# A second table of early tiles, a shorter row prefetch, and a new order of the first loads, in an attention-then-experts kernel

## The chip, the cores and the metric

The kernel runs on one core of one Trainium2 chip, in one launch. The metric is the device time in microseconds (us) of that core. TensorE does the matrix products, VectorE (DVE), ScalarE (ACT) and GpSimd (POOL) the elementwise work, and the SyncE queue (SP) issues most of the DMA transfers; GpSimd issues the indirect ones.

## The reference

Two stages follow each other. First a linear attention with a polynomial sketch:

```python
q_p, k_p = phi(q), phi(k)                 # phi: outer product of two 8-wide projections, 64 features
kv  = einsum('bhsf,bhsd->bhfd', k_p, v)
z   = sum(k_p, axis=2)
attn = einsum('bhsf,bhfd->bhsd', q_p, kv) / (einsum('bhsf,bhf->bhs', q_p, z)[..., None] + 1e-6)
```

with 4 batches, 4 heads, 1088 positions and head size 32. Its output is laid out as 4352 rows x of 128 numbers. Then a mixture of 8 experts, in which each row goes to one expert alone:

```python
e_idx  = argmax(x @ w_gate, axis=1)
gate_w = softmax(x @ w_gate)[e_idx]
out[mask e] = gate_w * sigmoid(x @ w_output_gate)[e] * (relu(x[mask e] @ w1[e]) @ w2[e])
```

w1[e] is 128 x 1024 and w2[e] is 1024 x 128. All is in 32-bit floats.

## The kernel before

**Attention and routing.** The 34 chunks of 128 positions form 9 groups (of 4 chunks, the last of 2). A list of stage names written out by hand, PLAN, sets the program order of everything up to the first expert tiles: each word such as `qa4` or `rd2` calls a small function for one group or route. The groups are bundled in five routes, ROUTES = ((0, 1), (2, 3), (4, 5), (6,), (7, 8)). When a route's attention output is there, stage rc chooses the expert of each row, rp and rs work out a row number in a buffer xs in HBM, and rd (function send) scatters the rows there, one indirect DMA for each chunk (L544). In xs every expert has a region of its own, in which its rows stand in order of arrival. Each row of xs carries 128 numbers, its gate factor and the number of its output row. At the end, stage mp scatters padding rows behind the last row of each expert (L796), so that tiles can be whole.

**Expert tiles.** The experts work on tiles of TS = 128 rows of one expert. Which rows and which expert a tile has is data, so small tables are computed on DVE: eti (expert of each tile) and bti (its first row in xs). SyncE reads a table entry into a register (L626) and issues `rows(t)`, one DMA from xs into a buffer of the ring xin (L632), and `weights(t, a)`, 512 KB each, a = 0 for w1 and a = 1 for w2, into one of NW = 3 buffer pairs wt (L639). The weights are not loaded when the tile three places earlier had the same expert.

**Early tiles.** A tile that is full before all rows have been routed can be started before the end of the attention. The table early_tiles, made behind the second route (MARK = 1, stages mn1 and mt1), holds NE = 9 such tiles: 16 chunks have been routed, and whatever the distribution over the experts, nine tiles are full. Their `rows` need not wait for the later scatters. This is said by groups of instructions that are declared free of dependence on one another ("early"). All other tiles are in the table late_tiles, made behind the last route (mn4, mt4), and their rows wait for every scatter and for the padding. At mt1 the six weight loads of tiles 0 to 2 are issued, and then the nine `rows`.

**The pipeline of tiles.** Five stages make a tile on TensorE and its helpers: tx transposes xin (L803), tv copies the result out of PSUM (L808), tu multiplies by w1 in 16 matmuls (L815), th applies relu (L822), td multiplies by w2 in 16 matmuls (L829), ty scales (L839), and to scatters the tile to the output (L844). Program order on TensorE, once PLAN is done, is that of `step_(t)`:

```python
for w, n in (("tx", t + 2), ("tv", t + 2), ("tu", t + 1), ("th", t + 1), ("td", t), ("ty", t), ("to", t)):
```

Loads are issued where buffers come free: behind tu(t) the first half of the weights of tile t + 3, behind td(t) the second half of the weights of tile t + 3, and then the rows of tile t + NX, NX = 5. SyncE executes its queue in this order, so an entry that waits holds up all that stands behind it. The order in PLAN in which TensorE gets the first tiles is tx0, tx1, tx2, tu0, tx3, tu1, tx4, td0.

Of the kernel before, what the change touches and what calls it, by code (L numbers as in the profile page):

```python
# [13 lines left out]
F32 = mybir.dt.float32  # L14
I32 = mybir.dt.int32
ALU = mybir.AluOpType
# [6 lines left out]
NK, NV, NQ = 4, 5, 2  # L23
TS = 128
NW = 3
NX = 5

# [5 lines left out]
    gt1 qt3 gs1 ql1 gm1 qz1 qc3 ks6 rc0 gc1 ks8 kb6 qa3 kb8 kp6 rg0 rp0 qr3 qt2 rs0 rf0 qs4 qc2 qx3 rd0 kc5 qb4 ql3  # L35
    qp4 kc6 qa2 cl2 qz3 gt2 qr2 kp8 qt4 gs2 qx2 gm2 qc4 qs5 ql2 qz2 gc2 ks7 rc1 qb5 qa4 kb7 qp5 rp1 rg1 kc6 qr4 rs1
    qt5 rf1 mn1 kp7 qs7 qc5 rd1 mt1 qb7 kc7 kc8 qs6 qx4 qb6 ql4 qp6 qa5 cl3 qp7 gt3 qr5 qt6 gs3 qx5 gm3 qc6 qs8 ql5
    qz4 gc3 qt7 qb8 qz5 rc2 qa6 qc7 qa7 qr6 qp8 rg2 qx6 rp2 qr7 ql6 qx7 qt8 ql7 qc8 tx0 rs2 tx1 qa8 tv0 tv1 rf2 tx2
    qr8 tu0 tv2 rd2 qx8 ql8 qz8 tx3 th0 tu1 tv3 qz7 qz6 rc3 tx4 th1 td0 tv4 rg3 rp3 tu2 ty0 rs3 rf3 rc4 td1 th2 rg4
    mn4 tu3 mt4 ty1 rd3 td2 th3 tu4 ty2 rf4 rp4 th4 tx5 rs4 tx6 td3 tv5 tv6 rd4 mp4  # L40
"""
ROUTES = ((0, 1), (2, 3), (4, 5), (6,), (7, 8))
MARK = 1
NOWHERE = 1 << 20


# [5 lines left out]
def kernel(  # L52
# [12 lines left out]
    nc = tc.nc  # L65
# [3 lines left out]
    DM = H * D  # L69
    E = w_d.shape[0]  # L70
# [8 lines left out]
    W = DM + 16  # L79
    CAP = N + TS  # L80
    NT = (N + E * (TS - 1)) // TS
    PR = E * TS // 128

    consts = ctx.enter_context(tc.tile_pool(name="consts", bufs=1))
# [10 lines left out]
    def ring(pool, tag, n, shape):  # L95
        turns[tag] = [pool.tile(shape, F32, tag=f"{tag}{i}", name=f"{tag}{i}") for i in range(n)], [0]

    def nxt(tag):
        bufs, at = turns[tag]
        at[0] += 1  # L100
        return bufs[at[0] % len(bufs)]
# [11 lines left out]
    def apart(group, ins, *others):  # L113

        for g in (group,) + others:
            tc.declare_no_dep(ins.ins, group=g, reason="the rows are distinct")
        tc.add_to_no_dep_group(group, ins.ins)
# [7 lines left out]
    for i, x in enumerate((S1, S2)):  # L125
        own = slice(i * r, (i + 1) * r)
        if wide:
            x, dst, n = x.bitcast(I32), bits[own].rearrange("p d w -> p (d w)"), 2 * D
        else:
            dst, n = plain[own], D  # L130
# [55 lines left out]
    def half(a):  # L186
        return slice(a * FC * 128, (a + 1) * FC * 128)
# [21 lines left out]
    ones = consts.tile([128, 128], F32, tag="ones")  # L209
# [16 lines left out]
    routes = [range(groups[r[0]][0], groups[r[-1]][-1] + 1) for r in ROUTES]  # L226
# [2 lines left out]

    NE = -(-((routes[MARK][-1] + 1) * 128 - E * (TS - 1)) // TS)
    assert 0 < NE <= NT
    ring(consts, "xsT", 3, [128, TS])
    ring(consts, "hT", 2, [128, FC, TS])
    ring(consts, "y", NE + 1, [TS, DM])
    ring(consts, "xin", NE + NX + 2, [TS, W])
    eps = consts.tile([128, 1], F32, tag="eps")
    nc.gpsimd.memset(eps, EPS)
    fresh = {}  # L240
# [15 lines left out]
    pad = consts.tile([128, PR, W], F32, tag="pad")  # L256
# [19 lines left out]
    stepT = consts.tile([128, NT], F32, tag="stepT")  # L276
# [261 lines left out]
    def send(i, ey, sloti, co):  # L538
        n = len(routes[i])
        x = xts.pop(i)  # L540
        nc.gpsimd.tensor_copy(x.bitcast(I32)[:, :n, DM + 1], ids[:, routes[i][0]:routes[i][-1] + 1])
        nc.gpsimd.tensor_mul(x[:, :n, DM], co[:, :n], ey[:, :n, E + 1])  # L542
        for j in range(n):
            apart("rows", nc.gpsimd.indirect_dma_start(  # L544
                out=xs[:, :], out_offset=bass.IndirectOffsetOnAxis(ap=sloti[:, j:j + 1], axis=0),
                in_=x[:, j], in_offset=None, bounds_check=E * CAP - 1), *(["early"] if i > MARK else []))


    eti = consts.tile([128, NT], I32, tag="eti")
    bti = consts.tile([128, NT], I32, tag="bti")  # L550

    def spread(t, n):
        return t[:, :E].unsqueeze(1).to_broadcast((128, n, E))

    def table(t0, n, ends, jump, first, last=None):


        past = consts.tile([128, n, E], F32, tag=f"past{t0}", name="past")
        et = consts.tile([128, n], F32, tag=f"et{t0}", name="et")
        nc.vector.tensor_tensor(past, step[:, :n].unsqueeze(2).to_broadcast((128, n, E)), spread(ends, n), op=ALU.is_ge)  # L560
        with nc.allow_low_precision("numbers of experts are whole"):
            nc.vector.tensor_reduce(eti[:, t0:t0 + n], past[:, :, :E - 1], axis=AX, op=ALU.add)
        nc.vector.tensor_mul(past, past, spread(jump, n))
        nc.vector.tensor_reduce(et, past[:, :, :E - 1], axis=AX, op=ALU.add)
        if last is None:
            nc.vector.tensor_tensor(bti[:, t0:t0 + n], et, stepT[:, :n], op=ALU.add)
        else:

            nc.vector.scalar_tensor_tensor(out=et, in0=et, scalar=first, in1=stepT[:, :n], op0=ALU.add, op1=ALU.add)
            nc.vector.tensor_scalar(bti[:, t0:t0 + n], et, last, None, op0=ALU.min)  # L570

    NS = N // TS
    more = consts.tile([128, 1], I32, tag="more")
    done = consts.tile([128, E + 1], F32, tag="done")
    nc.vector.memset(done, 0.0)
    early = consts.tile([128, E + 1], F32, tag="early")
    nc.vector.memset(early, 0.0)

    def counted():
        ps = psum.tile([128, E], F32, tag="rt", name="ps_n")  # L580
        nc.tensor.matmul(ps, ones, state["carry"], start=True, stop=True)
        return ps

    def early_tiles(ps):
        full = consts.tile([128, E], I32, tag="full")
        jump = consts.tile([128, E], F32, tag="jump")
        nc.vector.tensor_tensor(full, ps, ecap, op=ALU.subtract)
        nc.vector.tensor_single_scalar(full, full, TS.bit_length() - 1, op=ALU.logical_shift_right)
        nc.vector.tensor_tensor_scan(done[:, 1:], ones[:, :E], full, 0.0, op0=ALU.mult, op1=ALU.add)
        nc.vector.tensor_scalar_min(done[:, 1:], done[:, 1:], float(NE))  # L590
        nc.vector.tensor_sub(early[:, :E], done[:, 1:], done[:, :E])
        nc.vector.tensor_scalar(jump, early[:, :E], -float(TS), float(CAP), op0=ALU.mult, op1=ALU.add)
        table(0, NE, done[:, 1:], jump, None)

    def late_tiles(ps):
        num = consts.tile([128, E], F32, tag="num")
# [17 lines left out]
        nc.vector.tensor_tensor_scan(ends, ones[:, :E], nt, 0.0, op0=ALU.mult, op1=ALU.add)  # L614
        nc.vector.tensor_single_scalar(more, ends[:, E - 1:], float(NS - NE), op=ALU.subtract)
        nc.vector.tensor_tensor(jump, early[:, 1:], left, op=ALU.subtract)
# [6 lines left out]
    regs, xin, xTs, hTs = {}, {}, {}, {}  # L623

    def value(tab, t, top):
        return nc.values_load(tab[0:1, t:t + 1], engines=[mybir.EngineType.SP], min_val=0, max_val=top,  # L626
                              skip_runtime_bounds_check_because="the table is made within the bounds")

    def rows(t):
        at = value(bti, t, E * CAP - TS)  # L630
        xin[t] = nxt("xin")
        ins = nc.sync.dma_start(xin[t], xs[bass.ds(at, TS), :])  # L632
        if t < NE:
            tc.add_to_no_dep_group("early", ins.ins)

    def weights(t, a):
        if a == 0:
            regs[t] = value(eti, t, E - 1)
        nc.sync.dma_start(wt[t % NW][a].rearrange("p c x -> p (c x)"),  # L639
                          w_d[bass.ds(regs[t], 1), :, half(a)].rearrange("e p x -> p (e x)"),  # L640
                          cond=regs[t] != regs[t - NW] if t >= NW else None)
# [12 lines left out]
    stages, have, did = {}, {}, set()  # L654
    end = [NT]
# [116 lines left out]
    @stage  # L772
    def rd(i):
        send(i, have.pop(("rg", i)), have.pop(("rs", i)), have.pop(("rf", i)))
# [4 lines left out]

    @stage  # L780
    def mt(i):
        if i == MARK:
            early_tiles(have.pop(("mn", i)))
            for t in range(NW):
                weights(t, 0)
                weights(t, 1)
            for t in range(NE):
                rows(t)
        else:
            late_tiles(have.pop(("mn", i)))  # L790

    @stage
    def mp(i):
        pa, pai = have.pop("pai")
        nc.gpsimd.tensor_copy(pai, pa)
        apart("rows", nc.gpsimd.indirect_dma_start(  # L796
            out=xs[:, :], out_offset=bass.IndirectOffsetOnAxis(ap=pai[:, :1], axis=0),
            in_=pad.rearrange("p a b -> p (a b)"), in_offset=None), "early")

    @stage  # L800
    def tx(t):
# [22 lines left out]
    @stage  # L824
    def td(t):
        hT = have.pop(("th", t))
        ps = have["td", t] = nxt("kvz").rearrange("p a x -> p (a x)")[:, :DM]
        for c in range(FC):
            nc.tensor.matmul(ps, hT[:, c], wt[t % NW][1][:, c], start=(c == 0), stop=(c == FC - 1))  # L829
        if t + NW < end[0]:  # L830
            weights(t + NW, 1)
        if t + NW >= NE - 1:
            for n in range(NE if t + NW == NE - 1 else t + NX, min(t + NX + 1, end[0])):
                rows(n)

    @stage
    def ty(t):
# [85 lines left out]
```

## Time and profile before

The time is 250.34 us, the median of three runs (250.05 to 256.19). The profiled execution has a span of 224.9 us.

| | |
|---|---|
| PE busy | 200.6 us, 89% of the span |
| PE weight loads busy | 194.9 us, 87% |
| DVE / ACT / POOL busy | 31% / 33% / 35% |
| mean granted TensorE clock | 0.958 |
| DMA | 49.10 MB, mean 218 GB/s |
| of it the hardware queue q1 | 43.31 MB in 19,024 packets |
| L815 matmuls | 592, 76.0 us; 592 more on L829, 72.5 us |
| weight loads issued / row fetches issued | 79 / 41 |

37 tiles are worked on, so 592 = 37 x 16. Each busy time adds up the recorded durations of an engine's instructions; a share is a mean over stages that have different limits, so the chain of waits and the timeline are needed to see where time could go. The span is cut into 40 slices, and TensorE's clock falls to half in two places beside the end: in the slices at 62 to 67 us, where the expert tiles begin, and at 101 to 107 us.

### The profile page before, as it was taken

How to read it: one execution, taken by the hardware profiler on the slowest of the kernel's cores; microseconds unless marked ns; L12 is line 12 of the kernel's file. 1: busy time of each engine (PE TensorE's matmuls, PEld its weight loads, DVE VectorE, ACT ScalarE, POOL GpSimd, SP SyncE). 2: the span in 40 equal slices, each digit the busy share in tenths (PEclk: the TensorE clock that was granted, in tenths of full speed). 3: DMA queues.
4: the chain of work that ended last, by engine and by line, in shares of the span. 5: the costliest groups of instructions: out<-in, count | busy, mean ns of one | idle time of the engine just before them, and what ended most of it. 6: DMA issues, size and time to landing. Idle time of an engine off the chain costs nothing.

```text
span 224.9 us, 6588 instructions
## 1 busy us (share of the span) xinstructions
PE 200.6 (89%) x2458; PEld 194.9 (87%) x2458; DVE 69.3 (31%) x221; ACT 74.0 (33%) x140; POOL 78.8 (35%) x130
## 2 busy tenths in 40 slices
PE   7899999999489999907999999999999999999720
PEld 6889999998379999907999999999999999999720
DVE  4557889999645670000000010101010101010000
ACT  2123343425204343400434343433434343434300
POOL 3700006777037747771131313132222223131310
PEclk9999999999958999995999999999999999999995
DMA  5866512349636989966898789989984686883100
GB/s 160 315 193 225 155 50 77 115 117 357 247 94 175 319 294 282 312 254 197 251 315 322 227 237 319 313 314 312 330 311 143 207 263 189 269 292 114 38 30 1
DMA packets 21634, 49.10 MB, mean 218 GB/s; under 512 B 3466, under 2 KB 9100, under 8 KB 21600
## 3 DMA queue, kind: packets, MB, share of 16 engines
q1 hardware_dynamic: 19024, 43.31, 60.2%
q0 software_dynamic: 2416, 5.33, 6.3%
q8 instruction: 21, 0.34, 0.7%
q14 instruction: 13, 0.11, 0.2%
q10 hardware_dynamic: 160, 0.01, 0.0%
HBM read 51.17 MB, written 5.52 MB: 252 GB/s over the span
## 4 chain that ended last, share of the span: by engine, by line
PE 56%; DMA 22%; issue 9%; POOL 7%; DVE 1%; SPq 0%; POOLq 0%; ACT 0%
PE w L815 22%; PE kvz L829 18%; DMA out_dram<-y,xin 12%; POOL xs L544 7%; PE t L346 5%; DMA xs<-pad,pai 4%; PE w L430 2%; PE kvz L405 2%; DMA xs<-x,sloti 2%; DMA wt<-in_w_dram 2%; DMA xin<-xs 2%; PE t L803 2%; PE w L322 2%; PE w L416 1%; DVE kp L362 1%
## 5 line engine op out<-in xcount | busy, mean ns | idle before, releaser
L815 PE MATMUL w<-xsT,wt 128*128 128x128 f32 x592 | 76.0, 284 | 0.0
L829 PE MATMUL kvz<-wt,hT 128*128 128x128 f32 x592 | 72.5, 276 | 1.5 <-SPq L875 1.5
L815 PEld LDWEIGHTS w<-xsT,wt 128*128 128x128 f32 x592 | 72.8, 201 | 0.0
L829 PEld LDWEIGHTS kvz<-wt,hT 128*128 128x128 f32 x592 | 69.5, 193 | 1.7 <-issue 1.7
L844 POOL DMA_INDIRECT out_dram<-y,xin x37 | 35.9, 970 | 88.1 <-DMA wt<-in_w_dram 46.4
L822 ACT ACTIVATE hT<-w 128x1024 f32<-128x1024 f32 x37 | 37.9, 1023 | 69.2 <-PE w L815 69.2
L808 DVE COPY xsT<-t 128x128 f32<-128x128 f32 x38 | 11.0, 291 | 121.9 <-PE t L803 121.9
L544 POOL DMA_INDIRECT xs<-x,sloti x34 | 33.7, 990 | 12.2 <-issue 8.8
L839 ACT ACTIVATE y<-kvz,xin 128x128 f32<-128x128 f32 x37 | 13.6, 367 | 28.6 <-PE kvz L829 28.6
L803 PE MATMUL t<-ident,xin 128*128 128x128 f32 x38 | 11.0, 295 | 10.3 <-DMA xin<-xs 10.3
L803 PEld LDWEIGHTS t<-ident,xin 128*128 128x128 f32 x38 | 5.6, 150 | 11.1 <-DMA xin<-xs 10.9
L430 PE MATMUL w<-kz,qpT 128*64 128x98 f32 x272 | 13.8, 256 | 0.4 <-ACT b_sb L354 0.4
L430 PEld LDWEIGHTS w<-kz,qpT 128*64 128x64 f32 x272 | 12.4, 142 | 0.9 <-ACT b_sb L354 0.5
L542 POOL TENSOR_TENSOR x<-co,ey 128x8 f32<-128x8 f32 (+2 forms) x5 | 1.1, 223 | 33.5 <-DVE rc L447 23.7
L422 ACT COPY qpT<-w 128x1024 f32<-128x1024 f32 (+1 forms) x9 | 8.7, 965 | 9.9 <-PE w L416 9.9
L362 DVE TENSOR_TENSOR qp<-t,b_sb 128x1024 f32<-128x1024 f32 (+1 forms) x9 | 10.4, 1160 | 3.0 <-ACT b_sb L354 2.8
L362 DVE TENSOR_TENSOR kp<-t,b_sb 128x1024 f32<-128x1024 f32 (+1 forms) x9 | 10.4, 1160 | 2.9 <-PE kvz L405 1.8
L405 PE MATMUL kvz<-vt,kp 128*64 128x65 f32 (+1 forms) x288 | 10.5, 223 | 0.0
L346 PE MATMUL t<-Sb,kT 128*64 128x64 f32 x272 | 9.8, 224 | 0.8 <-DVE kp L362 0.5
L354 ACT COPY b_sb<-t 128x128 f32<-128x128 f32 (+1 forms) x18 | 4.7, 259 | 16.4 <-PE t L346 16.1
L346 PEld LDWEIGHTS t<-Sb,kT 128*64 128x64 f32 x272 | 8.7, 138 | 1.6 <-DVE kp L362 0.6
L405 PEld LDWEIGHTS kvz<-vt,kp 128*64 128x64 f32 (+1 forms) x288 | 9.4, 137 | 0.5 <-issue 0.2
(130 smaller groups left out, 120.8 us busy)
## 6 DMA issues: line engine op xcount, KB each, us to landing
wt<-in_w_dram SPq DMA_DIRECT2D x79, 512.0 KB
xin<-xs SPq DMA_DIRECT2D x41, 72.0 KB
vt<-in_v_dram SPq DMA_DIRECT2D x8, 260.0 KB
kT<-in_k_dram SPq DMA_DIRECT2D x8, 256.0 KB
qT<-in_q_dram SPq DMA_DIRECT2D x8, 256.0 KB
out_dram<-y,xin POOLq DMA_INDIRECT x37, 4.7
xs<-x,sloti POOLq DMA_INDIRECT x34, 4.4
vt<-in_v_dram SPq DMA_DIRECT2D x1, 130.0 KB
```

Of the source, the lines that this page charges most:

```text
L346: nc.tensor.matmul(ps[64 * t:64 * (t + 1), j * H:(j + 1) * H], src[:, j * 128 + 64 * t:j * 128 + 64 * (t + 1)], Sb[i], start=i == 0 and j ...
L362: nc.vector.tensor_mul(res[:, :n], bview(av, [list(av.ap[1]), list(av.ap[2]), [0, r]]), bview(bv, [list(bv.ap[1]), [0, r], list(bv.ap[2])]))
L405: nc.tensor.matmul(acc[b][64 * h:64 * (h + 1), s], kp[p0:p0 + np_, j * H + 2 * s + h].rearrange("s i j -> s (i j)"), vt[p0:p0 + np_, j, s] ...
L430: nc.tensor.matmul(ps[64 * t:64 * (t + 1), 2 * j + s, :VG], qpT[:, 2 * j + s, 64 * t:64 * (t + 1)], kz[(c * 128 + 64 * t) // S][:, s], sta ...
L544: apart("rows", nc.gpsimd.indirect_dma_start(out=xs[:, :], out_offset=bass.IndirectOffsetOnAxis(ap=sloti[:, j:j + 1], axis=0), in_=x[:, j] ...
L803: nc.tensor.transpose(have["tx", t], xin[t][:, :DM], ident)
L808: nc.vector.tensor_copy(have["tv", t], have.pop(("tx", t)))
L815: nc.tensor.matmul(ps[:, c], wt[t % NW][0][:, c], xT, start=True, stop=True)
L822: nc.scalar.activation(have["th", t], have.pop(("tu", t)), ACTF.Relu)
L829: nc.tensor.matmul(ps, hT[:, c], wt[t % NW][1][:, c], start=(c == 0), stop=(c == FC - 1))
L839: nc.scalar.activation(have["ty", t], have.pop(("td", t)), ACTF.Copy, scale=xin[t][:, DM:DM + 1])
L844: apart("out", nc.gpsimd.indirect_dma_start(out=out, out_offset=bass.IndirectOffsetOnAxis(ap=x.bitcast(I32)[:, DM + 1:DM + 2], axis=0), in ...
```

## The change

A second table of early tiles is made behind the third route (stages mn2 and mt2, MARKS = (1, 2)). After 24 chunks, 17 tiles are full, so tiles 9 to 16 come from this table and need only the scatters of the first three routes. The late table holds what is left. The groups of independent instructions become early0 and early1, one for each table. NX goes from 5 to 4, so that the rows of tile 17, the first of the late table, are asked for just behind the weights of tile 16. At mt1 the loads are issued tile by tile: both weight halves of tile t, for t below 3, and then its rows. So the weights of tiles 1 and 2 now stand in SyncE's queue behind the first row fetch and its wait. The rings y and xin grow from 10 to 14 and from 16 to 20 buffers, and three tables are cleared on GpSimd where two were cleared on DVE.

```diff
-NX = 5
+NX = 4
-    ... tx0 rs2 tx1 qa8 tv0 tv1 rf2 tx2
-    qr8 tu0 tv2 rd2 qx8 ql8 qz8 tx3 ...
+    ... tx0 rs2 mn2 tx1 qa8 tv0 tv1 rf2 tx2
+    qr8 tu0 tv2 rd2 mt2 qx8 ql8 qz8 tx3 ...
-MARK = 1
+MARKS = (1, 2)
-    NE = -(-((routes[MARK][-1] + 1) * 128 - E * (TS - 1)) // TS)
+    NES = [-(-((routes[m][-1] + 1) * 128 - E * (TS - 1)) // TS) for m in MARKS]
+    NE = NES[-1]
-    ring(consts, "y", NE + 1, [TS, DM])
-    ring(consts, "xin", NE + NX + 2, [TS, W])
+    ring(consts, "y", 14, [TS, DM])
+    ring(consts, "xin", 20, [TS, W])
@@ send @@
-                in_=x[:, j], in_offset=None, bounds_check=E * CAP - 1), *(["early"] if i > MARK else []))
+                in_=x[:, j], in_offset=None, bounds_check=E * CAP - 1), *(f"early{k}" for k, m in enumerate(MARKS) if i > m))
@@ early_tiles: 16 DVE instructions in place of 11 @@
+        t0, t1 = ([0] + NES)[k:k + 2]
+        was, now = earlies[k:k + 2]
...
+        nc.vector.tensor_tensor(new, full, was[:, :E], op=ALU.subtract)
...
+        nc.vector.tensor_add(now[:, :E], was[:, :E], new)
+        nc.vector.tensor_tensor(jump, was[:, 1:], now[:, :E], op=ALU.subtract)
+        nc.vector.tensor_scalar(jump, jump, float(TS), float(CAP), op0=ALU.mult, op1=ALU.add)
+        nc.vector.tensor_scalar_mul(first, was[:, :1], float(TS))
+        table(t0, t1 - t0, ends[:, 1:], jump, first)
@@ rows @@
-        if t < NE:
-            tc.add_to_no_dep_group("early", ins.ins)
+        for k, n in enumerate(NES):
+            if t < n:
+                tc.add_to_no_dep_group(f"early{k}", ins.ins)
@@ mt @@
-        if i == MARK:
-            early_tiles(have.pop(("mn", i)))
-            for t in range(NW):
-                weights(t, 0)
-                weights(t, 1)
-            for t in range(NE):
+        if i in MARKS:
+            early_tiles(MARKS.index(i), have.pop(("mn", i)))
+        if i == MARKS[0]:
+            for t in range(NES[0]):
+                if t < NW:
+                    weights(t, 0)
+                    weights(t, 1)
                 rows(t)
@@ td @@
-        if t + NW >= NE - 1:
-            for n in range(NE if t + NW == NE - 1 else t + NX, min(t + NX + 1, end[0])):
-                rows(n)
+        if NES[0] <= t + NX < end[0]:
+            rows(t + NX)
```

More of the change, by code (lines that the diff above doesn't have):

```diff
@@ L37 @@
     qt5 rf1 mn1 kp7 qs7 qc5 rd1 mt1 qb7 kc7 kc8 qs6 qx4 qb6 ql4 qp6 qa5 cl3 qp7 gt3 qr5 qt6 gs3 qx5 gm3 qc6 qs8 ql5
-    qz4 gc3 qt7 qb8 qz5 rc2 qa6 qc7 qa7 qr6 qp8 rg2 qx6 rp2 qr7 ql6 qx7 qt8 ql7 qc8 tx0 rs2 tx1 qa8 tv0 tv1 rf2 tx2
-    qr8 tu0 tv2 rd2 qx8 ql8 qz8 tx3 th0 tu1 tv3 qz7 qz6 rc3 tx4 th1 td0 tv4 rg3 rp3 tu2 ty0 rs3 rf3 rc4 td1 th2 rg4
+    qz4 gc3 qt7 qb8 qz5 rc2 qa6 qc7 qa7 qr6 qp8 rg2 qx6 rp2 qr7 ql6 qx7 qt8 ql7 qc8 tx0 rs2 mn2 tx1 qa8 tv0 tv1 rf2 tx2
+    qr8 tu0 tv2 rd2 mt2 qx8 ql8 qz8 tx3 th0 tu1 tv3 qz7 qz6 rc3 tx4 th1 td0 tv4 rg3 rp3 tu2 ty0 rs3 rf3 rc4 td1 th2 rg4
     mn4 tu3 mt4 ty1 rd3 td2 th3 tu4 ty2 rf4 rp4 th4 tx5 rs4 tx6 td3 tv5 tv6 rd4 mp4
@@ L228 @@
     RG = max(len(rs) for rs in routes)
-    NE = -(-((routes[MARK][-1] + 1) * 128 - E * (TS - 1)) // TS)
-    assert 0 < NE <= NT
+    NES = [-(-((routes[m][-1] + 1) * 128 - E * (TS - 1)) // TS) for m in MARKS]
+    NE = NES[-1]
+    assert 0 < NES[0] and NE <= NT
     ring(consts, "xsT", 3, [128, TS])
     ring(consts, "hT", 2, [128, FC, TS])
-    ring(consts, "y", NE + 1, [TS, DM])
-    ring(consts, "xin", NE + NX + 2, [TS, W])
+    ring(consts, "y", 14, [TS, DM])
+    ring(consts, "xin", 20, [TS, W])
     eps = consts.tile([128, 1], F32, tag="eps")
@@ L565, in table @@
         if last is None:
-            nc.vector.tensor_tensor(bti[:, t0:t0 + n], et, stepT[:, :n], op=ALU.add)
+            nc.vector.scalar_tensor_tensor(out=bti[:, t0:t0 + n], in0=et, scalar=first, in1=stepT[:, :n],
+                                           op0=ALU.add, op1=ALU.add)
         else:
@@ L573 @@
     more = consts.tile([128, 1], I32, tag="more")
[L574 to L577, printed above, removed]
+    earlies = [consts.tile([128, E + 1], F32, tag=f"early{k}", name=f"early{k}") for k in range(len(MARKS) + 1)]
+    for x in earlies:
+        nc.gpsimd.memset(x, 0.0)
+    early = earlies[-1]
     def counted():
@@ L582, in counted, with early_tiles @@
         return ps
-    def early_tiles(ps):
-        full = consts.tile([128, E], I32, tag="full")
-        jump = consts.tile([128, E], F32, tag="jump")
+    def early_tiles(k, ps):
+        t0, t1 = ([0] + NES)[k:k + 2]
+        was, now = earlies[k:k + 2]
+        full = consts.tile([128, E], I32, tag=f"full{k}", name="full")
+        new = consts.tile([128, E], F32, tag=f"new{k}", name="new")
+        ends = consts.tile([128, E + 1], F32, tag=f"ends{k}", name="ends")
+        jump = consts.tile([128, E], F32, tag=f"jump{k}", name="jump")
+        first = consts.tile([128, 1], F32, tag=f"first{k}", name="first")
         nc.vector.tensor_tensor(full, ps, ecap, op=ALU.subtract)
+        nc.vector.memset(ends[:, :1], 0.0)
         nc.vector.tensor_single_scalar(full, full, TS.bit_length() - 1, op=ALU.logical_shift_right)
[L589 to L593, printed above, removed]
+        nc.vector.tensor_tensor(new, full, was[:, :E], op=ALU.subtract)
+        nc.vector.tensor_tensor_scan(ends[:, 1:], ones[:, :E], new, 0.0, op0=ALU.mult, op1=ALU.add)
+        nc.vector.tensor_scalar_min(ends[:, 1:], ends[:, 1:], float(t1 - t0))
+        nc.vector.tensor_sub(new, ends[:, 1:], ends[:, :E])
+        nc.vector.tensor_add(now[:, :E], was[:, :E], new)
[3 more added lines that the diff above has]
+        table(t0, t1 - t0, ends[:, 1:], jump, first)
     def late_tiles(ps):
@@ L781, in mt @@
     def mt(i):
-        if i == MARK:
-            early_tiles(have.pop(("mn", i)))
-            for t in range(NW):
-                weights(t, 0)
-                weights(t, 1)
-            for t in range(NE):
+        if i in MARKS:
[5 more added lines that the diff above has]
+                    weights(t, 1)
                 rows(t)
-        else:
+        elif i not in MARKS:
             late_tiles(have.pop(("mn", i)))
@@ L797, in mp @@
             out=xs[:, :], out_offset=bass.IndirectOffsetOnAxis(ap=pai[:, :1], axis=0),
-            in_=pad.rearrange("p a b -> p (a b)"), in_offset=None), "early")
+            in_=pad.rearrange("p a b -> p (a b)"), in_offset=None), *(f"early{k}" for k in range(len(MARKS))))
     @stage
```

## The prediction

> **What bounds the kernel now.** I read the chain that ended last first, because TensorE's 89% busy share is a mean over two halves with different limits. From tile 0 on (62 us) the chain is TensorE's own L815 and L829 work, 1.79 us each and 3.68 us a tile, with one break:
>
> ```profile
> 90.61 0.97 POOL xs L544
> 91.59 0.19 POOL pai L795
> 91.92 0.14 issue
> 92.06 8.63 DMA xs<-pad,pai
> 100.71 1.89 DMA xin<-xs
> 102.64 0.48 PE t L803
> 103.12 3.41 PE w L815 x16
> 106.53 2.04 PE kvz L829 x16
> 108.57 0.11 PE t L803
> 108.68 1.79 PE w L815 x16
> 110.47 1.79 PE kvz L829 x16
> ```
>
> See there: the nine early tiles run out, the first late row tile (tile 9) may be fetched only when the pad scatter has landed (100.71), and TensorE, which ended its last L829 at 95.85 by the timeline, starts again at 102.64. The next tile then costs 3.41 + 2.04 instead of 1.79 + 1.79. The list of waits confirms who waited:
>
> ```profile
> PEld t L803 <- DMA xin<-xs: 10.9, 3, 7.0
> PE t L803 <- DMA xin<-xs: 10.3, 3, 6.8
> ```
>
> Three waits in all: one of 6.8 us here, two of 3.5 us together at the start (62 to 63 us). In the whole steady part, rows are never waited for. How much room they have is in the timeline, which I read next:
>
> ```profile
> 109.45 0.33 SPq L632 DMA_DIRECT2D xin<-xs  x1
> ...
> 110.30 1.95 PE L829 MATMUL kvz<-wt,hT 128*128 128x128 f32 x16
> ...
> 112.09 0.27 PE L803 MATMUL t<-ident,xin 128*128 128x128 f32 x1
> ...
> 113.12 0.33 SPq L632 DMA_DIRECT2D xin<-xs  x1
> ...
> 115.77 0.27 PE L803 MATMUL t<-ident,xin 128*128 128x128 f32 x1
> ```
>
> Stage td of tile 7 ends at 108.57; 0.9 us later SyncE issues the rows of tile 12 (NX = 5), and the transpose of tile 12 is the L803 at 115.77: 6.3 us of room. The L829 at 110.30 is td of tile 8, ending at 112.25; under NX = 4 it is behind this one, at 113.12, that tile 12's rows would go out: 2.65 us of room.
>
> How long they take I read from the trace's DMA packet records. Row packets are the only ones of 576 bytes, 128 a tile, so the end of each tile's last packet can be told:
>
> ```
> rows of tile   issued    last packet ends   took
>  9 (queue empty) 100.71     102.31           1.6
> 12               109.45     113.42           4.0
> 18               131.60     135.60           4.0
> 19 to 26, mean                               4.5
> 28, 29, 30 (tiles 27, 28 load nothing)       2.8, 2.2, 1.9
> 31               179.47     183.25           3.8
> ```
>
> TensorE started 0.35 us after the last packet where it waited (tiles 0, 1 and 9).
>
> **What the Trainium skill says.** "DMA: Bandwidth & Descriptors", section "Queues, rings and completion order": a DMA from SyncE is spread over rings on the 16 engines, and on each engine its descriptors are taken in ring order. So rows issued just behind 512 KB of weights queue behind them on every engine. The trace agrees: 1.6 us with an empty queue, 1.9 to 2.8 around tiles that load nothing, about 4 or more behind two loads. "TensorE: Matmul & The Clock Gate", Part 1: after an idle window of about 3.4 us TensorE drops to half clock. The trace agrees: 3.41 us for sixteen L815 after the gap. The same DMA page's "Specifications" put HBM at about 358 GB/s a core; this trace's windows show up to 412 GB/s from 56 to 58 us, so the measurement decides, but the steady 312 to 330 GB/s of the page's slices is not far from full, as engines are about 94% busy from 131 to 166 us.
>
> **The change part by part.**
>
> *Second table (17 early tiles).* Tiles 9 to 16 need only routes 0 to 2, whose last scatter is issued at about 74.3 us; scatters land 2.3 to 6.3 us after issue (the view of tile xs), so before td of tile 5 asks for tile 9 (about 92 us). Tile 17's rows are asked for by td of tile 13, at the earliest 95.85 + 7 x 3.68 = 121.6 us, 21 us after the pad scatter landed; even doubled, its 8.6 us are hidden. The gap goes: 6.8 us of idle, and (3.41 - 1.79) + (2.04 - 1.79) = 1.9 us of slow clock. **-8.7 us.**
>
> *Its DVE work.* early_tiles has 16 DVE instructions where it had 11; those took 2.4 us (45.75 to 48.14), 0.22 each, so a table now costs about 3.5 us. At mt1 this delays the first weights by 1.1 us; they have until 64.8 us, so nothing. At mt2 the 3.5 us stand on DVE ahead of ql8, which frees the PSUM buffer that tu1 writes; DVE has 4.5 us idle between 62 and 70 us, but not all of it in that place.
>
> *Order of the first loads.* Today 3 MB of weights precede the wait for the scatters, and the scatter issued at 54.87 lands only at 60.15, 5.3 us later. With 1 MB ahead I take the least landing that the trace shows, 2.3 us: rows 0 out at 57.2 and at TensorE 1.9 us later, 59.1, just when its earlier work ends (59.14). But now 1 MB of weights goes ahead of rows 1 and another ahead of rows 2, and tx2 stands before tu0 in the plan. 1 MB at some 350 GB/s (the page's slice at 50 to 56 us, 357) is 3.0 us; SyncE issues each load 0.6 us and each row fetch 0.8 us after the one before, and the first bytes come about 1.2 us after issue. That makes rows 1 ready at about 63.3 and rows 2 at 66.3, against 62.9 and 64.8. tu0 starts 1.7 us later; part of it falls out of the half-clock stretch, and mt2 then holds tu1: td0 ends about 2 us later than now. **+2.0 us** (0 to 3.5).
>
> *NX from 5 to 4.* This is the large term. Call lag the time from the end of td(t) to the last packet of the rows it asks for: 0.9 us to issue plus 3.8 to 4.5, that is 4.7 to 5.4 us with both weight halves loading. The path: td(t) frees a weight buffer, SyncE issues 512 KB into it, then the rows behind it in the ring; tx(t+4) is first on TensorE after td(t+1), with tu(t+3) and td(t+2) queued behind. So lag + 0.35 must fit one step of 3.68 us plus that step's own stall. If each step stalls s, then lag + 0.35 = (3.68 + s) + s, so s = (lag + 0.35 - 3.68) / 2. Lag 4.2, 4.7 and 5.4 give 0.43, 0.69 and 1.03 us. I take 0.7, near the lower measured lag: a stalled TensorE asks for weights less often, so the backlog falls towards that of a load begun on an idle ring (tiles 12, 18, 31). The lowest bound is an empty queue, lag 0.9 + 1.6 = 2.5, and s = 0. It concerns tiles 9 to 36, 28 steps: **+19.6 us** (12 to 29). Stalls under 1.5 us leave no 3.4 us idle window, so I charge no clock.
>
> *Weights reloaded.* A load is skipped when the tile three earlier has the same expert. Listing the tiles from the inputs' gating gives five skips now (64 loads of 512 KB for 37 tiles, 33.6 MB; with q, k, v and rows 43.3 MB, which is the 43.31 MB of the page's hardware queue q1), and one after (72 loads), since three tables split each expert's run. 4.2 MB more by DMA; no time of its own, but the breathing spells around tiles 15, 27, 28 and 32 vanish.
>
> *Rings.* xin 20 and y 14: their waits are on scatters 20 and 14 tiles back, which the timeline shows done. The added memsets move to GpSimd, which does nothing that is waited for then. Nothing.
>
> Sum: -8.7 + 2.0 + 19.6 = +12.9 us. The profiled span (224.9) lies below the timed 250.34; I carry the difference over as fixed: **263.2 us**.
>
> **Rivals.**
> - *Rows stay hidden.* If rows land within 3.3 us of td's end, the gap's gain stands alone: 250.3 - 8.7 + 2.0 = 243.6, faster. For it: an unloaded fetch takes 1.6 us, and nothing waits for rows now. Against it: the ring order, and no full-load tile under 3.8 us.
> - *The stalls heal half.* Each stall drains the rings; lag 4.0 gives s = 0.33, 9.4 us: 250.3 - 8.7 + 2.0 + 9.4 = 253.0. Against it: tiles 12, 18 and 31 began on drained rings and still had lags of 4.7 to 5.0.
> - *DMA becomes the bound.* With no light tiles and route scatters in the same rings, lag stays 5.4 or more and some stalls cost clock: s = 1.1, 30.8 us: 274. Against it: DMA load falls when TensorE stalls.
>
> **How the numbers follow.** Forecast 0.68, hidden rows 0.14, half healed 0.12, DMA-bound 0.06. The forecast spans s of 0.4 to 1.0, 255 to 272 us. Leaving out the hidden case and the far end, the range is 248 to 274. Faster by over 2% is the hidden case, 0.14; within 2% is the half-healed one, 0.11; the rest, 0.75, is slower.
>
> **What would show it.** Right: no gap near 96 us, no half clock there; "PE t L803 <- DMA xin<-xs" with some 28 waits of 0.4 to 1.5 us, 15 to 25 us in total; 4.2 MB more on q1; L803 alternating with idle on the chain. The first-loads step: row fetches at 57 us, then transposes 0, 1, 2 some 3 us apart. Wrong if those waits stay under 5 us in total from tile 9 on, with 3.68 us from transpose to transpose; then the fetch behind the weights is faster than the packets of now say.

## The result, and the profile after

The changed kernel takes **278.73 us** (median of 4 runs, 276.4 to 280.93) where the kernel before took 251.59 (4 runs, 250.05 to 256.19): a ratio of **1.107, 95% interval 1.090 to 1.124**. It is slower, as forecast, and by twice as much as forecast: +27 us instead of +12.9, and outside the range of 248 to 274.

These are the lines of the changed kernel's page that answer to those of before: the busy times, the clock in 40 slices, the hardware queue, the chain by engine, and the group of the transposes (L819 is what L803 was).

```profile
PE 217.3 (79%) x2460; PEld 204.2 (74%) x2460; DVE 72.1 (26%) x240; ACT 73.5 (27%) x140; POOL 79.2 (29%) x133
...
PEclk9999997795797999777999999999999999999965
...
q1 hardware_dynamic: 20032, 47.43, 55.3%
...
issue 38%; PE 23%; DMA 12%; POOL 11%; DVE 6%; another core or an unknown queue 4%; POOLq 1%; ACT 1%; DVEq 0%; ACTq 0%
...
L819 PE MATMUL t<-ident,xin 128*128 128x128 f32 x38 | 11.6, 311 | 21.8 <-DMA xin<-xs 21.7
```

TensorE is busy 79% of 274.7 us instead of 89% of 224.9. Queue q1 moved 47.43 MB instead of 43.31: the eight more weight loads (4.19 MB) less one row fetch (0.07). In front of the transposes TensorE now waits 21.7 us for rows. The list of waits says in how many pieces:

```profile
PEld t L819 <- DMA xin<-xs: 26.0, 22, 2.3
PE t L819 <- DMA xin<-xs: 21.7, 20, 2.1
```

Twenty waits of at most 2.1 us stand where there were three, one of them of 6.8. TensorE's timeline shows their rhythm (start, duration, line, and in brackets the idle time before and who ended it):

```profile
132.54 0.33 PE L819 MATMUL t<-ident,xin 128*128 128x128 f32 x1 [1.40 <-DMA xin<-xs]
132.70 1.96 PE L831 MATMUL w<-xsT,wt 128*128 128x128 f32 x16
134.50 1.95 PE L845 MATMUL kvz<-wt,hT 128*128 128x128 f32 x16
136.29 0.32 PE L819 MATMUL t<-ident,xin 128*128 128x128 f32 x1
136.44 1.96 PE L831 MATMUL w<-xsT,wt 128*128 128x128 f32 x16
138.24 1.95 PE L845 MATMUL kvz<-wt,hT 128*128 128x128 f32 x16
141.34 0.33 PE L819 MATMUL t<-ident,xin 128*128 128x128 f32 x1 [1.15 <-DMA xin<-xs]
```

From transpose to transpose it is 3.75 us, then 5.05: a short step, a long one, and so on to the end. From the end of td of tile 6 (126.7 us) to that of tile 36 (265.1) these 30 steps take 138.3 us; at 3.68 each they would take 110.5. That is **27.8 us** above full speed; the kernel before is 8.9 us above it in the same steps, all of it at its gap ahead of tile 9. But a second thing in this trace hides what else happened. Ahead of tile 6 TensorE drips, with nothing that the profile names in between:

```profile
57.89 0.31 PE L406 MATMUL kvz<-vt,kp 128*64 128x65 f32 x3 [0.37 <-issue]
58.60 0.35 PE L406 MATMUL kvz<-vt,kp 128*64 128x65 f32 x3 [0.41 <-issue]
59.33 0.37 PE L406 MATMUL kvz<-vt,kp 128*64 128x65 f32 x4 [0.38 <-issue]
60.07 0.36 PE L406 MATMUL kvz<-vt,kp 128*64 128x65 f32 x4 [0.37 <-issue]
```

Such stretches stand at 57 to 67 us, ahead of the first transpose, which starts only at 79.5 us, and again at 84, 111 and 117 us. They do not come from the change alone: in this series the kernel before took some 250 us too, while on three other chips it took 226 us in every series. On one of these the same changed kernel took 260 us, with none of these stretches. Whether the chip or something else about this series makes them was not tested. The experiments were compared on the other chips.

### The profile page after: what moved, and what is told of

It reads as the page before. It is cut to its first block, busy times and chain, and to the rows that moved or that the text cites. A ratio compares the mean times of both kernels' runs of the same rounds, so it can differ in the third digit from the quotient of the medians.

```text
span 274.7 us, 6605 instructions
## 1 busy us (share of the span) xinstructions
PE 217.3 (79%) x2460; PEld 204.2 (74%) x2460; DVE 72.1 (26%) x240; ACT 73.5 (27%) x140; POOL 79.2 (29%) x133
## 3 DMA queue, kind: packets, MB, share of 16 engines
q1 hardware_dynamic: 20032, 47.43, 55.3%
## 4 chain that ended last, share of the span: by engine, by line
issue 38%; PE 23%; DMA 12%; POOL 11%; DVE 6%; another core or an unknown queue 4%; POOLq 1%; ACT 1%; DVEq 0%; ACTq 0%
DMA out_dram<-y,xin 12%; POOL out_dram L859 9%; PE t L347 6%; PE w L831 4%; PE kvz L406 4%; PE w L431 2%; POOL xs L545 2%; PE w L417 1%; PE kvz L845 1%; PE w L323 1%; DVE qp L363 1%; DVE x L449 1%; PE ps_kg L391 1%; POOLq L859 1%
## 5 line engine op out<-in xcount | busy, mean ns | idle before, releaser
L845 PE MATMUL kvz<-wt,hT 128*128 128x128 f32 x592 | 76.5, 285 | 5.6 <-issue 2.8
L845 PEld LDWEIGHTS kvz<-wt,hT 128*128 128x128 f32 x592 | 72.8, 201 | 6.2 <-issue 5.1
L831 PEld LDWEIGHTS w<-xsT,wt 128*128 128x128 f32 x592 | 71.7, 197 | 5.3 <-issue 5.3
L819 PE MATMUL t<-ident,xin 128*128 128x128 f32 x38 | 11.6, 311 | 21.8 <-DMA xin<-xs 21.7
L819 PEld LDWEIGHTS t<-ident,xin 128*128 128x128 f32 x38 | 5.4, 144 | 26.2 <-DMA xin<-xs 26.0
L406 PE MATMUL kvz<-vt,kp 128*64 128x65 f32 (+1 forms) x288 | 14.1, 230 | 5.8 <-issue 5.8
L406 PEld LDWEIGHTS kvz<-vt,kp 128*64 128x64 f32 (+1 forms) x288 | 11.2, 140 | 8.1 <-issue 7.8
L431 PE MATMUL w<-kz,qpT 128*64 128x98 f32 x272 | 15.5, 266 | 1.0 <-issue 1.0
L431 PEld LDWEIGHTS w<-kz,qpT 128*64 128x64 f32 x272 | 13.7, 150 | 1.9 <-issue 1.6
L347 PE MATMUL t<-Sb,qT 128*64 128x64 f32 x272 | 11.5, 246 | 0.0
L347 PE MATMUL t<-Sb,kT 128*64 128x64 f32 x272 | 10.5, 235 | 0.9 <-DVE kp L363 0.6
```

The source lines that it names most:

```text
L347: nc.tensor.matmul(ps[64 * t:64 * (t + 1), j * H:(j + 1) * H], src[:, j * 128 + 64 * t:j * 128 + 64 * (t + 1)], Sb[i], start=i == 0 and j ...
L406: nc.tensor.matmul(acc[b][64 * h:64 * (h + 1), s], kp[p0:p0 + np_, j * H + 2 * s + h].rearrange("s i j -> s (i j)"), vt[p0:p0 + np_, j, s] ...
L431: nc.tensor.matmul(ps[64 * t:64 * (t + 1), 2 * j + s, :VG], qpT[:, 2 * j + s, 64 * t:64 * (t + 1)], kz[(c * 128 + 64 * t) // S][:, s], sta ...
L819: nc.tensor.transpose(have["tx", t], xin[t][:, :DM], ident)
L831: nc.tensor.matmul(ps[:, c], wt[t % NW][0][:, c], xT, start=True, stop=True)
```

## The experiments

My theory: the shorter row prefetch (NX) makes the slow steps; the second table closes the gap at tile 9; the new order of the first loads delays the start a little. The rivals: the slow steps come from the eight more weight loads or a full DMA; the gap was never closed; the load order costs more than it seems. This table has the ends of td for tiles 0, 6 and 36 from each trace, so start, gap and steady part can be told apart. The 30 steps between the last two take 110.5 us if TensorE is never held up.

| run | time us | td 0 | td 6 | td 36 | 6 to 36, over 110.5 |
|---|---|---|---|---|---|
| before again | 226.02 | 72.65 | 95.60 | 214.66 | 8.6 |
| after again | 260.04 | 76.11 | 99.06 | 247.63 | 38.1 |
| after, NX = 5 | 229.29 | 78.06 | 101.01 | 218.84 | 7.3 |
| before, NX = 4 | 251.87 | 73.23 | 96.18 | 242.03 | 35.4 |
| after, rows ahead of weights | 234.96 | 76.03 | 98.98 | 223.30 | 13.8 |
| rows ahead of route 4 | 225.06 | 77.33 | 102.04 | 214.71 | 2.2 |
| the same, old load order | 223.04 | 73.68 | 98.38 | 210.03 | 1.2 |
| after, NX = 5, old load order | 225.07 | 74.08 | 97.03 | 213.78 | 6.3 |
| before, new load order | 229.65 | 75.70 | 98.64 | 218.59 | 9.4 |
| table later | 223.29 | 73.42 | 101.85 | 213.68 | 1.3 |
| both mends once more | 222.05 | 73.72 | 100.63 | 212.69 | 1.6 |
| table later, four weight buffers | 221.09 | 72.96 | 97.99 | 208.50 | 0.0 |

The last column does not show all: from td 0 to td 6 seven of the runs take 22.9 us, but the five with rows ahead of route 4 (that one, and the four made from it) take 24.7 to 28.4, as new waits came up there.

**Before again** (no edit).

> The kernel before, unchanged, for a second profile. Its first profile has a span of 224.9 us, but its timed runs take 250. If the timed runs hold stalls that the first profile lacked, this one has a span of 245 to 252 us, td of tile 6 ends some 20 to 25 us later than 95.85, and the steps from tile 9 on are 3.68 us as before. If the difference is a fixed cost outside the span, the span is again 223 to 227 us.

226.02 us against 226.03 (7 runs, 224.83 to 227.6), with a span of 224.3 us. There is no difference of 25 us here, so this run could not tell where it lies. The first profile already held the answer: its own execution took 226.58 us for a span of 224.9. The gap is there: 8.6 us over 110.5, so the -8.7 of the prediction was the right size for what there was to gain.

**After again** (no edit, on the second of the other chips).

> After, unchanged, beside before on a chip where before takes 226 us. If the cost of the change is the stalls of NX = 4 (28 us) plus a few us at the start, less what the late gap hides, this takes 251 to 256 us: the same 26 to 28 us more than before as on the first chip, where both were some 25 us longer. If the first chip's extra 25 us belonged to the change, it takes under 240.

260.04 us (258.89 to 264.04) against 225.82: ratio 1.150, 1.138 to 1.162. That is 34 us more than before, and outside the 251 to 256 us that I expected. Without the dripping, the gap that the second table was to close stands open. SyncE's own waits in this run, and the chain around the issue of the pad scatter:

```profile
SPq L645 <- DMA xs<-pad,pai: 7.3, 1, 7.3
SPq L645 <- DMA xs<-x,sloti: 6.6, 1, 6.6
```

```profile
94.78 0.20 POOL pai L811
94.98 0.04 issue
95.03 0.03 POOLq L859
95.06 0.05 issue
95.10 0.02 POOLq L859
95.12 0.14 issue
95.26 6.11 DMA xs<-pad,pai
```

A row fetch (L645) still waits 7.3 us for the pad scatter, although the trace's records show it is that of tile 9, an early tile now: td of tile 5 ended at 95.38, the pad scatter, issued at 95.26, landed at 103.57, and SyncE issued the rows at 103.59. Compare before: 8.63 us of "DMA xs<-pad,pai", then rows at 100.71.

**The changed kernel with the old prefetch distance.**

```diff
-NX = 4
+NX = 5
```

> After, with NX = 5 alone set back. Theory A (rows asked for one step later land behind the weights and stall TensorE every step): the steps after tile 9 go back from 4.61 to 3.68 us over 30 steps, 28 us less than after, 248 to 252 us, and no wait for rows from tile 9 on. Theory B (the loss is in the start: order of the first loads, second table on DVE): still over 268 us. Theory C (72 weight loads in place of 64 make DMA the bound): steps stay above 4.2 us, over 265 us.

229.29 us (227.71 to 230.25), ratio 1.012, 1.003 to 1.020. One number takes back 30.7 us of the 34, as theory A expected (27 to 31). The steady steps are as before, with all 72 loads:

```profile
128.96 0.27 PE L819 MATMUL t<-ident,xin 128*128 128x128 f32 x1
129.07 1.95 PE L831 MATMUL w<-xsT,wt 128*128 128x128 f32 x16
130.86 1.95 PE L845 MATMUL kvz<-wt,hT 128*128 128x128 f32 x16
132.65 0.27 PE L819 MATMUL t<-ident,xin 128*128 128x128 f32 x1
```

3.69 us from transpose to transpose and no bracket. The rows are no quicker (the last packet ends 5.5 us after td, the median over tiles 9 to 36), they have a whole step more. So the DMA is not the bound, and the eight more loads take no time of their own in these steps. The gap is here too, against the expectation of no wait for rows from tile 9 on: SyncE waits 8.2 us for the pad.

**The old kernel with the short prefetch.**

```diff
-NX = 5
+NX = 4
```

> Before, with NX = 4 alone. Theory A: 27 steps of late tiles that stall 0.85 to 0.95 us each, 23 to 26 us more than before, 273 to 278 us. Theory B: no difference, 250 us. Theory C: the weight loads are those of before (64), so no difference or a few us, under 256.

251.87 us (247.54 to 253.39) against 226.03: +25.8 us by the medians, +21.5 by its fastest run, from this one number and with nothing else of the change. Its steps from tile 9 to 36 take 4.59 us on average, short and long ones mixed, where the kernel before takes 3.69. Both directions agree, so the slow steps are NX's.

**Rows ahead of weights.** In the changed kernel with NX = 4, td asks for the rows first and then for the second half of the weights.

```diff
+        if NES[0] <= t + NX < end[0]:
+            rows(t + NX)
         if t + NW < end[0]:
             weights(t + NW, 1)
-        if NES[0] <= t + NX < end[0]:
-            rows(t + NX)
```

> After, NX = 4 kept, but td issues the rows of tile t + 4 ahead of the second weight half of tile t + 3 instead of behind it, so they neither wait for td nor stand behind its 512 KB. Theory A: the last row packet comes 2 to 3 us after td ends in place of 4.9, which is within one step, so the stalls go: 248 to 254 us, steps of 3.7 to 3.8 us. Theory B: as after, over 268. Theory C: as after, over 265.

234.96 us (233.98 to 239.26), ratio 1.038, 1.028 to 1.047; that is 25 us less than the changed kernel. My numbers were in the scale of the first chip (278.7), so the difference is what to compare. SyncE's timeline:

```profile
119.99 0.33 SPq L645 DMA_DIRECT2D xin<-xs  x1
120.93 2.23 SPq L653 DMA_DIRECT2D wt<-in_w_dram  x2
123.79 0.33 SPq L645 DMA_DIRECT2D xin<-xs  x1
124.61 2.23 SPq L653 DMA_DIRECT2D wt<-in_w_dram  x2
127.36 0.33 SPq L645 DMA_DIRECT2D xin<-xs  x1
```

The rows need no buffer that td frees (xin has 20), so they may go out before td is done: by the packet records (medians of tiles 10 to 35) they are issued 0.85 us ahead of td's end and not 0.93 us behind it. The edit also puts them in front of one load in the ring, but that shows no gain: from issue to last packet they take 4.2 us, against 3.9 in after again. So the 25 us come from asking 1.8 us sooner, with the same bytes. From td's end to the last row packet it is 3.4 us in place of 4.9, more than the 2 to 3 expected, and the steps from tile 9 on take 3.96 us. Ten waits remain, 13.3 us with those at the start and at tile 9.

**Rows of the second table ahead of the later scatters.** If tile 9 waits for the pad because of its place in the program, then rows issued ahead of route 3's scatters (rd3) must not wait. NX is 5.

```diff
-    mn4 tu3 mt4 ty1 rd3 td2 ...
+    mn4 tu3 mt4 ty1 er2 rd3 td2 ...
+    def er(i):
+        k = MARKS.index(i)
+        for t in range(NES[k - 1], NES[k]):
+            rows(t)
-        if NES[0] <= t + NX < end[0]:
+        if NE <= t + NX < end[0]:
```

> After with NX = 5, and the rows of tiles 9 to 16 issued in the program ahead of the scatters of the fourth route (stage er2), so that they cannot wait for those nor for the padding. Theory E (in after the rows of tile 9 still wait for the pad scatter, since an instruction that comes after it in the program keeps its dependence; the second table frees nothing): tile 9 follows tile 8 with no idle and no half clock, 5 to 6 us less than e1_after_nx5 (229.3), 222 to 225 us. Rival F (tile 9 waits for its own scatters, slow on full rings, and not for the padding): the gap stays, 227 to 230 us.

225.06 us (222.81 to 226.49), ratio 0.996, 0.993 to 0.998; 4.2 us below the changed kernel with NX = 5, where I expected 5 to 6. Rival F falls. SyncE's waits name no pad any more, and the rows of tiles 9 to 16 are in the core by 92.3 us, before they are needed and before the pad scatter is issued (96.5). SyncE's only wait on xs, and then TensorE where the gap was (td is L851 in this kernel, tu L837, tx L825):

```profile
SPq L645 <- DMA xs<-x,sloti: 6.6, 1, 6.6
```

```profile
92.86 1.95 PE L837 MATMUL w<-xsT,wt 128*128 128x128 f32 x16
96.34 2.02 PE L851 MATMUL kvz<-wt,hT 128*128 128x128 f32 x16 [1.52 <-DMA wt<-in_w_dram]
98.20 0.27 PE L825 MATMUL t<-ident,xin 128*128 128x128 f32 x1
```

No half clock there, but a new, small wait: with the gap closed, weights are late by 1.52 us. It ends ahead of td of tile 6. A wait of this size could not be seen behind the gap.

**The order of the first loads**, alone and together. The same edit, back to six weight loads and then nine row fetches, was made on the last kernel and on the changed one with NX = 5; its opposite was made on the kernel before.

```diff
+            for t in range(NW):
+                weights(t, 0)
+                weights(t, 1)
             for t in range(NES[0]):
-                if t < NW:
-                    weights(t, 0)
-                    weights(t, 1)
                 rows(t)
```

Old order, with the rows ahead of route 4:

> The same, and the six weight loads of tiles 0 to 2 ahead of the first row fetch as before. Theory G (in the new order, rows 1 and 2 queue behind 2 MB of weights and TensorE idles into half clock, 5.2 us at td of tile 0): td of tile 0 ends at 73 to 75 us in place of 78, 218 to 221 us in all. Rival H (the 5 us are the second table's work on DVE ahead of ql8): td of tile 0 still ends at 77 to 78, 222 to 225 us.

Old order in the changed kernel with NX = 5:

> After with NX = 5 and the old load order, rows of tile 9 where after has them. Under E and G the earlier start only lengthens the wait for the padding, which lands at the same time: td of tile 0 at 73 to 75 us, a gap ahead of tile 9 of 6 to 7 us, 226 to 228 us, as before. Under F or H it differs: under F 222 to 225.

New order in the kernel before:

> Before with the new order of the first loads alone (weights of tiles 1 and 2 behind the first row fetch). Theory G: td of tile 0 ends at 76 to 77 us in place of 72.7, and since tile 9 waits for the padding anyway the wait shrinks by about as much: 225 to 228 us in all. Rival H (the second table's DVE work made the late start): td of tile 0 at 72 to 74 us.

The old order ends the first td 3.7 us sooner in one pair (77.33 to 73.68) and 4.0 in the other (78.06 to 74.08); the new order ends it 3.0 later in the kernel before (72.65 to 75.70). So rival H falls: the order does it, with and without the second table. The times: 223.04 (221.19 to 224.86) against 225.06; 225.07 (ratio 0.997, 0.994 to 1.000) against 229.29; and 229.65 (ratio 1.014, 1.008 to 1.019). None of the three is in the range that I gave (218 to 221, 226 to 228, 225 to 228). In the kernel before I had expected the gap to swallow the delay, and there I was wrong: the rows of tile 9 went out later too, at 103.78 against 100.71 and 99.10 in its two traces with the old order, because the pad scatter moved with the rest (issued at 94.87 against 92.06 and 91.82). With NX = 5 in the changed kernel, the start reads so, and below it that of before again:

```profile
63.78 0.48 PE L819 MATMUL t<-ident,xin 128*128 128x128 f32 x1 [2.69 <-DMA xin<-xs]
67.21 0.45 PE L819 MATMUL t<-ident,xin 128*128 128x128 f32 x1 [1.45 <-DMA xin<-xs]
67.45 3.62 PE L831 MATMUL w<-xsT,wt 128*128 128x128 f32 x16
...
71.92 3.75 PE L831 MATMUL w<-xsT,wt 128*128 128x128 f32 x16 [0.63 <-issue]
```

```profile
64.95 3.62 PE L815 MATMUL w<-xsT,wt 128*128 128x128 f32 x16
...
68.58 2.18 PE L815 MATMUL w<-xsT,wt 128*128 128x128 f32 x16
```

Transposes 0, 1 and 2 start at 59.9, 63.8 and 67.2, each behind 1 MB: 3.9 and 3.4 us apart, a little more than the "some 3 us" forecast. But tu0 starts at 67.5, where before it started at 65, and with tu1 it runs at half clock (3.62 and 3.75 us); before, tu1 took 2.18. That tu1 is slow is not the rule: in after again and rows ahead of weights, with the same start, it takes 2.02 us, and the first td ends at 76.1 and 76.0 instead of 78.1.

**The second table's DVE work later**, behind tv3, on the kernel with both mends (rows ahead of route 4, old load order).

```diff
-    qr8 tu0 tv2 rd2 mt2 qx8 ql8 qz8 tx3 th0 tu1 tv3 qz7 ...
+    qr8 tu0 tv2 rd2 qx8 ql8 qz8 tx3 th0 tu1 tv3 mt2 qz7 ...
```

> As e5_and_old_load_order (223.0), with stage mt2 behind qz8 and tv3 in the plan, so that the 16 DVE instructions no longer stand ahead of ql8. What is left of the late start after the load order, 73.8 against 72.7 us at td of tile 0, is put down to them: td of tile 0 at 72.5 to 73.2, 222 to 223 us. If it is something else: 223 again and 73.8.

223.29 us (221.94 to 224.99), ratio 0.985, 0.981 to 0.989: no gain over 223.04. The first td ends 0.3 us sooner (73.42), short of the 72.5 to 73.2 expected. At 74.90 TensorE waits 1.48 us for DVE (L517 for oh), and a stretch of half clock follows from 76.72 to 80.13. That the moved table work causes the wait is likely and was not tested by itself.

**A fourth pair of weight buffers**, on top of that, loaded behind the first nine row fetches.

```diff
-NW = 3
+NW = 4
-            for t in range(NW):
+            for t in range(NW - 1):
...
+            weights(NW - 1, 0)
+            weights(NW - 1, 1)
```

> As e8_table_later, with NW = 4 pairs of weight buffers in place of 3, the fourth loaded behind the first nine row fetches. If the 1.5 us wait for weights near 94 us and its like come from short prefetch, 1 to 2 us less than e8; if DMA is full there anyway, the same within 1 us. 220 to 223 us.

221.09 us (219.91 to 222.49), ratio **0.978, 0.974 to 0.983**, the best, and 2.2 us below the run without the fourth pair. TensorE waits for no weights, and tiles 6 to 36 take 110.5 us: these steps are full from end to end.

**Both mends once more**, measured beside the last two.

> e5_and_old_load_order once more, in more rounds, for an interval: 222 to 224 us, 0.98 to 0.99 of before.

222.05 us (221.63 to 224.01), ratio 0.982, 0.978 to 0.986. One wait of 2.1 us for weights is left in it, such as the run with four buffers no longer has; the difference of 1.0 us between the two medians is small beside their scatter.

## Why the prediction was wrong in size and right in direction

On the other chips all terms can be read from one pair of traces, after again against before again, by the ends of td: 33.0 us in all.

| term | forecast | measured |
|---|---|---|
| start, to td of tile 6 | +2.0 | +3.5 |
| gap, td of tile 6 to td of tile 9 | -8.7 | +1.6 |
| steady steps, to td of tile 36, NX 4 | +19.6 | +27.9 |
| sum | +12.9 | +33.0 |

The gap's +1.6 is the three steps to td of tile 9 after (20.98 us) less those of before (19.33).

**"The gap goes": this step failed.** I worked out when the scatters of routes 0 to 2 land and took it that only they count, since early tiles are declared free of the later ones. But the rows of tiles 9 to 16 are still asked for in td of tiles 5 to 12, and that of tile 5 stands behind rd3, rd4 and mp4 in PLAN. The fetch behind the scatter waited for it, in spite of the declaration. The first nine tiles never showed this, as their fetches are all issued at mt1, ahead of the later scatters. Issuing tiles 9 to 16 early too removes the wait and 4.2 us (with NX = 5). So the place in the program decides; why the declaration does not free a fetch that comes later, no run shows. The second table thus closed no gap as it was built. On the first chip TensorE waited only 0.5 us for the rows of tile 9 and SyncE waited for no pad, as the dripping had held all up for longer; that may be why the ratio there is 1.107 and not 1.150, but it rests on one trace of that chip, and there is none of the kernel before in the same state.

**"NX from 5 to 4": mechanism right, three terms too small.** Two steps last from the end of td(t) to the end of td(t+2): lag, restart (from the last packet to the transpose), then from the start of the transpose to the end of td. I had 4.7 + 0.35 + 3.68 = 8.73 us. In the changed kernel's trace (tiles 10 to 35) the lag is 4.91, the restart 0.46 and the last part 3.91: the transpose, which otherwise begins before td has ended, stands alone after a stall. That is 9.28, or 4.64 a step, where I had 4.37; over 28 steps the three terms are short by 7.7 us. (That the steps measure 4.65 is no test of the sum, as the three make up two steps by their definition.) I had picked a low lag because the backlog would fall when TensorE stalls. It did: from issue to last packet the rows take 4.0 us on average, against 4.5 with NX = 5. But 4.0 and 0.95 to issue is still more than 4.7. So the largest of the three, 0.23 us, is the last part, which I took for a plain step.

**"I charge no clock" was partly wrong.** In the after-again trace two of the stalls, of 2.2 us, were each followed by a stretch of half clock, and those two steps took 7.7 us, some 2 us more than the other long ones (so clock makes some 4 of the 27.9 us, by my estimate from these steps):

```profile
145.42 0.33 PE L819 MATMUL t<-ident,xin 128*128 128x128 f32 x1 [2.21 <-DMA xin<-xs]
145.59 3.55 PE L831 MATMUL w<-xsT,wt 128*128 128x128 f32 x16
...
166.02 0.39 PE L819 MATMUL t<-ident,xin 128*128 128x128 f32 x1 [2.15 <-DMA xin<-xs]
166.20 3.57 PE L831 MATMUL w<-xsT,wt 128*128 128x128 f32 x16
```

"Stalls under 1.5 us" was the slip: a mean of 0.7 comes as 1.4 and 0, and some reach 2.2. That a stall must leave 3.4 us idle to cost clock was wrong too (see the last section).

**The order of the first loads:** direction right, and the fetches as forecast: rows 2 were in the core at 66.1 to 66.5 us in after again (packets of tile 3 mix in), where I had 66.3. But td of tile 0 moved by 3.0 to 4.0 us instead of 2.0. The term that was short is the start of tu0: in five traces with the new order transpose 2 began 0.9 to 1.5 us after the last packet of its rows, not 0.35. What holds it, no run shows. In after again tu1 then waited 1.0 us for relu; with NX = 5 half clock lasted longer instead.

**Weights reloaded and rings:** right as far as shown: 47.43 MB, and 3.68 us a step with all 72 loads as soon as NX is 5.

**The offset between timed and profiled:** I carried 25 us over as fixed. It is not outside the span: every profiled execution takes some 1.7 us more than its span (226.58 and 224.9 before, 276.4 and 274.7 after). The profile of before was of a quicker execution than the timed ones, and the changed kernel's profile on the first chip has stalls inside its span. What makes them no run settled.

**The rivals:** "rows stay hidden" falls by the two NX runs. "The stalls heal half" falls by the lag of 4.9. "DMA becomes the bound" is wrong in its reason, as all 72 loads fit into full steps with NX = 5, but its stalls that cost clock came true, and its 30.8 us lie nearer to the measured 27.9 than my 19.6. On the other chips the forecast difference missed because one credit of 8.7 us was never paid and the main debt was short by 8 us; errors of the same sign add up. The sign that I had named, 15 to 25 us of waits for rows, was met by 21.7 us, and still the loss was larger (27.8 us in that trace), since these waits do not count what no longer overlaps after a stall.

## What to carry to other kernels

Before a prefetch distance is cut, add up what a fetch needs: the time to its issue, its time in the queue, the restart, and what the first operation no longer overlaps. Here that sum came to two steps and 1.9 us more, and each of the two steps paid half of the excess. A small fetch that stands behind bulk loads only because of where it is written can be asked for sooner; here 1.8 us sooner took 25 us off, and no matmul waited for weights in that run. A dependence that is declared away can still be waited for, so find out in the trace which instruction waits, and for what, before a gain is credited.

## What was not expected of the hardware

- **Half clock without a whole idle window.** "TensorE: Matmul & The Clock Gate", Part 1, of the Trainium skill puts the fall to half clock after an idle window of about 3.4 us, in windows that run free of the kernel. The windows agree with the clock records of these traces: in each of the fourteen, the changes of the clock lie whole multiples of 3.41 us apart (145.68 and 166.16 us in after again, the starts of two half-clock stretches, are six of them apart). The idle part does not agree, and the measurement decides. Cut at these times, the traces have 845 windows at full clock. In 45 of them TensorE's matmuls left 1.90 us or more idle, and half clock followed each time; in the other 800 they left at most 1.81 us, and half clock followed twice. So about 1.9 us idle inside one window were enough here (matmul ends are modelled, so the figure is rough).
- **Where a stall lies decides, not its length alone.** In after again the stalls of 2.21 and 2.15 us, and in the old kernel with NX = 4 those of 2.37 and 1.90, lie inside one such window each, and half clock followed (sixteen matmuls in 3.55 us instead of 1.96 in the first). Stalls of 2.12 us in the changed kernel and of 1.94 in the old one with NX = 4 were cut in two by the end of a window (at 167.96 and 229.96 us), and nothing followed; of one of 2.03 us, 1.72 lay in one window. As the windows run free of the kernel, which of the two happens is luck.
- **The restart varies.** From a tile's last row packet to its transpose it took 0.35 to 0.71 us where TensorE was waiting in the changed kernel, 0.46 on average, not the constant 0.35 that three waits of the kernel before had suggested; at the start, for tile 2, 0.9 to 1.5.
- **One series was slower by some 25 us.** The kernel before took 250 to 256 us in the first series and 223.9 to 228.1 on three other chips. In the one slow trace, that of the changed kernel, TensorE ran groups of one to seven matmuls with 0.3 to 0.9 us between them, ended by nothing that the profile records, and from 113 to 122 us DVE, ScalarE and SyncE had waits of 6 to 8 us for "remote", a source outside the profile, as well.
